# A new hand-written order for a kernel of sliding-window attention and a squared-ReLU feed-forward layer

## The chip, the cores and the metric

The kernel runs on one core of one Trainium2 chip. The metric is the device time of one execution in microseconds (us). Five engines have instruction queues of their own and run them strictly in order: PE (TensorE, matrix products and transposes), DVE (VectorE), ACT (ScalarE), POOL (GpSimd) and SP (SyncE, which only issues transfers here). An instruction that waits for another engine holds up everything behind it on its own engine. Transfers (DMA) are issued by SP, POOL and, once, ACT, and run beside the engines.

## What is computed

Four batches, eight heads, 768 positions, 64 values a head. A query sees the 128 positions up to itself and the first four positions, the sinks. The attention output is laid out as 3072 tokens of 512 values and goes through two products with a squared ReLU between them.

```python
B, H, S, D = q.shape                                   # 4, 8, 768, 64
scores = q @ k.transpose(0, 1, 3, 2) / np.sqrt(D)
pos = np.arange(S)
rel = pos[:, None] - pos[None, :]
keep = (pos[None, :] < 4) | ((rel >= 0) & (rel < 128))
scores = np.where(keep, scores, -1e9)
a = softmax(scores)
x = (a @ v).transpose(0, 2, 1, 3).reshape(B * S, H * D)  # 3072 x 512
h = x @ w_in                                             # 512 x 2048
return np.maximum(h, 0.0) ** 2 @ w_out                   # 2048 x 512
```

Inputs and output are 32-bit floats; the kernel multiplies in bf16.

## The kernel before

**A list of operations and a written order.** The program first builds a list of 946 operations, numbered from 0. An operation is a small function that emits one step: a group of matmuls, one vector or activation instruction, one transfer. It names the engines that may do it, the operations that it follows, and the on-chip rooms that it takes and reads. Nothing of the order is decided by the list. The order is a constant, `ORDER` (line 21), of 946 words, one for each operation. A word is the operation's number, then, where the first engine in the operation's own list is not meant, a letter (`d` DVE, `a` ACT, `g` POOL), then, where an operation may take its PSUM room from either of two pools, `+0` or `+1`. `Plan.run` walks the words from left to right:

```python
o.engine = names[word[-1]] if word[-1] in names else next(iter(o.engines))
for s in o.takes:
    if len(s.pools) > 1:
        s.pool = s.pools[int(chosen.pop(0))]
    s.room = free[s.pool].pop(0)
self.idle = DUMMIES.get(n, 0)
o.run(o.engine)
```

So the order of the words sets two things at once: the order in each engine's queue, and which operation inherits which room, since a room goes to the back of its pool's free list when its last reader has been emitted. Exchanging two neighbouring words of different engines changes no queue. The semaphore waits between engines are derived from the data and from the rooms, so a step that inherits a room waits for the reader that was last in it.

**Rooms.** PSUM has eight banks: the pools `att` and `den` have two rooms of two banks each. SBUF pools: `qr` 5 (loaded q and k), `qs` 6, `expm` 8 (exponentials and other short-lived tiles), `r` 3, `osb` 2 (output), `sg` 4, `u` 2.

**Fillers.** `DUMMIES` (below `ORDER`) gives a few operations extra matmuls on TensorE whose result is not used: 29 in the warm-up at the start (945, line 1363), 8, 10 and 4 ahead of the transposes 58, 63 and 64 (line 185), 3 each ahead of 83, 91 and 97.

**Stages.** The four batches run in a software pipeline: while TensorE works on the layers of batch b, the attention of batch b+1 is interleaved with them.

- *Constants.* DVE fills tiles: 944, 0, 1 (`fill_first`) and 2 (`fill_second`), the last two each three memsets at lines 233 to 235, for the even and the odd batches. POOL builds the identity, triangles and biases (3, 4, 5, line 254) and the head rows (6).
- *Batch 0, loads and head pairs.* q and k of four head pairs come on SP's queue (8 to 15) into `qr`. 7 and 16 to 18 load the sink values; 19, 20, 22, 23, 31 and 32 load v, 21 and 24 to 26 `w_in`, 33 to 36 `w_out`, all on POOL's queue. Each pair's k and q are cast (55, 56 for pair 0; 61, 62; 67, 68; 73, 74), transposed on TensorE (57, 58; 63, 64; 69, 70; 75, 76) and unloaded from PSUM (59, 60; 65, 66; 71, 72; 77, 78; lines 192 on ACT and 194 on DVE).
- *Attention of a token group* (256 positions; three groups per batch). Scores (lines 606 and 613; 83, 84, 91, 92 for group 0, 103, 104, 113, 114 for group 1 of batch 0), exponentials on ACT (line 634), masks on POOL (line 218) or DVE, values (line 682) and a normalisation on DVE (a reciprocal and the product of line 699). The sinks have scores and exponentials of their own (lines 572 and 580; 81, 82 for batch 0, 210, 211 for batch 1, 686, 687 for batch 3) and masked values (79).
- *Turning x.* In batches 0 and 1 TensorE transposes x (99, 101, line 731) and DVE or ACT copies it to `xT` (100, 102). In batches 2 and 3 q and k are loaded by tiles of 128 positions on POOL's queue (line 403; 668 and 669 are the last two q tiles of batch 3) and turned by transfers on SP (line 461; 680 to 683 for the last tiles of batch 3), and x is turned by transfers on SP too (line 713; 486 and 487 for tile group (2,1), 502 and 503 for (2,2), where (2,1) is group 1 of batch 2).
- *Layer 1.* Batch 0: plain products (line 763; 156 is the first), ReLU (line 775 on ACT, 777 on DVE) and square (786). From batch 1 on a block is done with seven products in place of eight: DVE makes sums of `xT` (line 852; 594 to 596 for batch 2), TensorE the products (line 894), DVE subtracts results from a kept copy (line 936; 583 and 585) and adds at the end (line 963; 578), ACT squares.
- *Layer 2.* Two tile groups of batch 0 go by plain products (line 984; 297 and 298 empty group (0,1)); the others by the same seven-product scheme, with sums of the activations on DVE (line 1207; 300 to 303 for group (0,2)) and products on TensorE (line 1233; 304 and 305 for that group). Results are emptied into `osb` and stored by SP. The last group of batch 3 has a form of its own, with three stores (line 1094 and below).

In batch 1 the scores of group 0 are 212 and 219, of group 1 230 and 237; 232, 234, 239 and 241 are masks of group 1, 235 its values. In batch 3, 700, 709 and 716 are values, 701 the normalisation of 700, 727 scores of group 2, 614 the kept copy and 616 a product of a layer-1 block.

## Time and profile before

| | |
|---|---|
| runs of the kernel before | 209.33, 210.71, 211.39 us |
| median of the three | 210.71 us |
| profiled execution, first to last instruction | 208.3 us |
| instructions in it | 5924 |
| bytes moved | 26.10 MB, mean 125 GB/s |
| granted TensorE clock | 1.000 |

The profile is of another execution than the three timed ones. Its page gives busy times per engine, the span in slices, the transfers by queue, the chain of work that ended last, and the costliest groups of instructions by line. A group reads: start time (in a timeline) or busy time, line, engine, operation, the tile that is written and the one that is read with shapes, count, and in brackets the idle time of that engine just before and what ended it. A table of stretches reads: stretch, then length and TensorE's busy time with its count, then weight loads, DVE, ACT and POOL in the same manner, then the granted clock, the mean share of the transfer engines and GB/s.

### The profile page before, as it was taken

The page shows a single profiled execution, that of the slowest core. Times are in us where ns is not written, and L with a number is a line of the kernel's source. Part 1 is how long each engine was busy: PE and PEld are TensorE (multiplying, and loading weights), DVE is VectorE, ACT ScalarE, POOL GpSimd, SP SyncE. Part 2 cuts the span into 40 slices and gives each one's busy share as a digit, 9 for nine tenths or more (in the row PEclk, how much of TensorE's full clock was granted, in tenths as well). Part 3 has the DMA queues.
Part 4 walks back from the last instruction along what each step waited for, and adds up shares of the span by engine and source line. Part 5 has one row for each costly group of instructions (what it writes and reads, how often), then busy time and mean ns, then how long its engine had stood idle before and what let it go on. Part 6 is the DMA issues. An engine that isn't in the chain of part 4 may idle for free.

```text
span 208.3 us, 5924 instructions
## 1 busy us (share of the span) xinstructions
PE 200.5 (96%) x2476; PEld 174.3 (84%) x2476; DVE 173.1 (83%) x318; ACT 135.9 (65%) x189; POOL 96.4 (46%) x138
## 2 busy tenths in 40 slices
PE   7989999999998999999999998999999999999993
PEld 7658997457986889989878987999888999998893
DVE  6759268867599998999999987999989598999933
ACT  2695888433749589999987047988856248693110
POOL 7999274599599976689356209000043000000000
PEclk9999999999999999999999999999999999999999
...
GB/s 190 260 184 207 173 196 215 166 146 142 261 68 148 131 172 137 181 162 121 154 116 220 109 96 134 148 3 0 50 14 145 50 5 113 88 3 0 50 54 201
DMA packets 93994, 26.10 MB, mean 125 GB/s; under 512 B 86800, under 2 KB 91408, under 8 KB 93968
## 3 DMA queue, kind: packets, MB, share of 16 engines
...
q10 hardware_dynamic: 184, 0.14, 0.2%
...
HBM read 27.30 MB, written 6.29 MB: 161 GB/s over the span
## 4 chain that ended last, share of the span: by engine, by line
PE 82%; DVE 5%; DMA 4%; SPq 3%; ACT 2%; issue 2%; DVEq 0%; ACTq 0%
PE py L1233 26%; PE pm L894 23%; PE pm L763 10%; PE py L984 7%; PE po L682 6%; PE ps L613 4%; DMA qr<-in_q_dram 3%; PE pt L507 2%; PE py L1094 2%; SPq L351 2%; DVE t L936 1%; PE px L731 1%; DMA xT<-xn_sb 1%; SPq L461 1%; ACT expm L634 1%
## 5 line engine op out<-in xcount | busy, mean ns | idle before, releaser
L634 ACT ACTIVATE expm<-ps 128x1024 bf16<-128x1024 f32 (+1 forms) x48 | 43.7, 953 | 7.7 <-PE ps L613 7.5
L218 POOL TENSOR_SCALAR_AFFINE_SELECT expm<-expm 128x512 bf16<-128x512 bf16 x34 | 22.7, 705 | 44.2 <-ACT expm L634 40.4
L894 PEld LDWEIGHTS <-w_in_sb 128*128 128x128 bf16 x384 | 32.2, 114 | 2.0 <-issue 1.9
L1233 PEld LDWEIGHTS <-gT_sb 128*128 128x128 bf16 x288 | 27.2, 98 | 4.7 <-issue 1.4
L917 ACT ACTIVATE gT_sb<-r 128x1024 bf16<-128x1024 bf16 x28 | 28.8, 1054 | 2.5 <-DVE r L963 2.3
L894 PE MATMUL pm<-xs,wi 128*128 128x256 bf16 (+1 forms) x288 | 29.2, 246 | 0.1
L192 ACT ACTIVATE osb<-py 128x256 f32<-128x256 f32 (+1 forms) x30 | 11.9, 399 | 25.0 <-PE py L1233 19.8
L936 DVE TENSOR_TENSOR t<-t,pm 128x512 f32<-128x512 f32 x36 | 23.8, 683 | 3.7 <-PE pm L894 2.9
L894 PEld LDWEIGHTS <-wi 128*128 128x128 bf16 x288 | 24.6, 114 | 1.0 <-DVE xs L852 0.4
L1233 PEld LDWEIGHTS <-sg 128*128 128x128 bf16 x216 | 20.3, 98 | 2.7 <-issue 0.5
L963 DVE CUSTOM_DVE_ANT_1 r<-pm,t 128x1024 bf16<-128x1024 f32 x18 | 21.8, 1218 | 0.5 <-PE pm L894 0.5
L763 PE MATMUL pm<-xT,w_in_sb 128*128 128x256 bf16 x192 | 22.0, 273 | 0.0
L763 PEld LDWEIGHTS <-w_in_sb 128*128 128x128 bf16 x192 | 20.6, 114 | 0.3 <-issue 0.2
L894 PE MATMUL pm<-xs,w_in_sb 128*128 128x256 bf16 (+1 forms) x192 | 19.9, 246 | 1.0 <-DVE t L936 1.0
L951 ACT ACTIVATE r<-pm 128x1024 bf16<-128x1024 f32 x16 | 16.3, 1022 | 4.9 <-DVE osb L194 2.3
L1233 PE MATMUL py<-w_out_sb,gT_sb 128*128 128x256 bf16 x144 | 18.7, 273 | 0.6 <-ACT expm L634 0.6
L1233 PE MATMUL py<-wt,sg 128*128 128x256 bf16 x144 | 18.7, 273 | 0.0
L1233 PE MATMUL py<-wt,gT_sb 128*128 128x256 bf16 x144 | 18.5, 273 | 0.0
L682 PEld LDWEIGHTS <-expm 128*128 128x128 bf16 x352 | 16.6, 97 | 1.9 <-issue 0.6
L682 PE MATMUL po<-v,expm 128*128 128x65 bf16 x352 | 17.8, 193 | 0.3 <-ACT expm L634 0.3
L699 DVE TENSOR_TENSOR xn_sb<-po,rc 128x512 bf16<-128x512 f32 (+1 forms) x28 | 17.2, 615 | 1.0
L984 PE MATMUL py<-w_out_sb,gT_sb 128*128 128x512 bf16 x64 | 14.8, 379 | 0.0
(104 smaller groups left out, 376.9 us busy)
## 6 DMA issues: line engine op xcount, KB each, us to landing
...
v<-in_v_dram POOLq DMA_DIRECT2D x24, 128.0 KB, 6.2
qn<-in_k_dram POOLq DMA_DIRECT2D x20, 128.0 KB, 6.1
qn<-in_q_dram POOLq DMA_DIRECT2D x20, 128.0 KB, 6.5
...
```

Of the source, the lines that this page charges most:

```text
L218: nc.gpsimd.affine_select(out=e_tile, in_=e_tile, compare_op=ALU.is_ge, fill=fill, base=i - 1, pattern=[[0, n], [1 if i else -1, 128]], ch ...
L634: nc.scalar.activation(out=x[:, :, o:512], in_=bank_t["s", b, s, m][:, :, o:512], func=AF.Exp, scale=scale)
L682: touch(("po", b, s, m0), e, nc.tensor.matmul(pv[:, i, h2, :], lhsT=lhsT, rhs=rhs, start=(n_ == 0), stop=(n_ == len(mms) - 1)), j)
L699: touch(("po", b, s, m0), e, nc.vector.tensor_tensor(out=xn_sb[:, 2 * s:2 * s + 2, 128 * (m0 + j0):128 * (m0 + j0 + nj)].rearrange("p i (j ...
L763: nc.tensor.matmul(pm[:, i, :], lhsT=w_in_sb[:, fb // 4, kb, fb % 4:512:4], rhs=xT[:, c0 // 256:(c0 + cw) // 256, kb, :], start=(kb == 0), ...
L894: touch(tag, e, nc.tensor.matmul(y[:, bk, i, :], lhsT=weights(name, f0 + i, a), rhs=rhs[:, a, :], start=fresh and i == 0 and a == 0, stop= ...
L917: nc.scalar.activation(out=d, in_=x, func=AF.Square)
L936: touch(tag, e, nc.vector.tensor_tensor(out=T["t"], in0=T["t"], in1=T["y"][:, bk], op=ALU.subtract), bk)
L951: touch(tag, e, nc.scalar.activation(out=r, in_=T["y"], func=AF.Relu), 0, 1)
L963: touch(tag, e, nc.vector._custom_dve(TENSOR_ADD_SAT, out=r.rearrange("p b n c -> p b (n c)"), in0=T["y"].rearrange("p b n c -> p b (n c)" ...
L984: touch((b, u), e, nc.tensor.matmul(pm[:, i, :], lhsT=gT_sb[:, fb, 128 * t:128 * t + 128], rhs=w_out_sb[:, fb, :], start=(fb == 0), stop=( ...
L1233: touch((b, u), e, nc.tensor.matmul(region(name), lhsT=x[:, i, :], rhs=w_[:, i, :], start=first and i == 0, stop=i == HB - 1, skip_group_c ...
```

## The change

Only the constant `ORDER` is replaced by another arrangement of the same 946 words. `DUMMIES`, all functions, tiles and pool sizes stay. In the new order:

- 66 operations go to another engine than before, all of them among DVE, ACT and POOL. Four masks go from DVE to POOL (232, 241, 497, 729) and four from POOL to DVE (265, 474, 499, 724). The casts 56 (DVE) and 74 (ACT) go to POOL; 61, 67, 68 go from DVE to ACT, 73 from ACT to DVE. The rest are unloads, copies, evacuations, ReLUs and squares that go between DVE and ACT, in both directions. DVE has 285 operations where it had 282, ACT 180 where it had 185, POOL 100 where it had 98; PE keeps 321 and SP 60.
- Of the 122 operations that choose a PSUM pool, 23 choose otherwise.
- Words move by a few places nearly everywhere. At the start, `fill_second` (2) moves from the fourth place of DVE's queue to between the normalisation 98 and the copy 102. TensorE transposes k of pair 1 (63) first, then k of pair 0 (57), q of pair 1 (64), q of pair 0 (58), and only then computes the first scores (83); before, it took pair 0, scores 83, then pair 1. On POOL's queue the casts 56 and 74 stand among the first loads.
- The masks 497, 490 and 492 stand ahead of the last q loads of batch 3 (668, 669) on POOL's queue, where the latter stood first;  on SP the turns of x (486, 487, 502, 503) change places with the turns of batch 3 (680 to 683). The subtractions 583 and 585 stand ahead of the sum 594 on DVE, where 594 stood between them.

The diff, cut to the lines at the start and around those places (the whole constant changes):

```diff
 ORDER = """
-944 0 1 2 7 8 9 10 11 12 13 14 15 16 17 18 945+0 3 5 19 20 21 6 79 22 23 24 25 55d 56d 57+0 58 59d 60a 83+0 85 103+1
-105 26 27 28 62d 61d 63+1 64 67d 68d 65a 69+0 70 71d 72d 66a 84+1 73a 74a 75+1 76 78d 91+0 86 77a 93 80 113+1 87+0
-92+1 89 94 95+0 97 115 88 90 96 98 114+1 99+0 101 117 100d 104+0 81+1 102d 107 82 4 29 106g 30 31 32 33 34 35 36 37 38
-39 40 41 42 43 44 45 46 127 47 48 49 50 116d 118d 108d 156+0 109+1 119+1 121 111 162+0 110 120 122 112 123+1 125 124d
...
-474g 669 670 499g 471 522 679 488+0+0 555 554 526 497d 484+1 557 491 489 671 492g 490g
-477+0 500+0 485 478 559 501 561 527+0 528 529d 563 562 493+0 565 558d 494 534 530 535 531d 566+0 567 532 533a 568d 569
-564 570 572 571 536 683 682 677 678 486 502 680 711+0+0 487 503 573 574d 537 538 539d 540 681 541 560 714 712 704+0+0
-580+0 581 576 577 582d 583 594 584 585 575a 705 707 688+0+0 713g 715g 706g 708g 689 691 578 586 587 626+1 627 588a
-628a 612+0 686+0 613 687 630 596 692 690 595 629 631 716+0 717 589a 614a 632 633 579a 634a 635a 615 590 616 597 617
...
+8 0 944 945+0 9 1 55d 5 10 3 11 62d 12 61a 63+0 65 57+0 4 13 7 64 56 59a 14 15 58 19 66 67a 60 20 69+0 73d 21 83+1 68a
+103+1 22 85 71 70 74 23 6 72 24 25 75+0 84+1 77 26 79 76 105 86 91+1 78 93 27 87+0 89 106 92+1 95+1 94 88 90 28 104+0
+97 99+0 80 96 98 2 114+1 101 107 113+1 81+0 29 102 100a 115 117 156+0 30 31 82 109+0 108d 116d 119+1 118d 32 111 110
+121 33 157 34 112 35 122 127 158a 162+1 120 36 163 123+0 125 124a 126 168+0 169 165+0 177+0 164a 37 38 39 166 40 174+1
...
+550 516 521 553 495+0+0 496 551 498 497 527+0 488+0+0 489 483d 491 481d 552d 474d 672 528 555 556 522 673 666 554
+484+0 558 678 561 490 529 685 525 485 562 477+0 492 674 557 564 534 478 563 493+0 530 499d 559 526 667 531d 500+0
+566+0 532 568 501 668 679 494 567 533d 570 486 711+0+0 502 569 535 537 669 571 572 536 573 714 565 538 715 712 503 683
+539 540 574 704+0+0 575 580+0 487 581 576 582d 705 707 682 584 583 585 688+0+0 594 680 577 595 586 689 691 587 626+1
+578 588 627 681 706 713 596 690 628 686+0 670 687 692 612+0 613 630 629 716+0 632 631 717 614 616 708 633 590 579a
...
```

The first removed line of the second part is the end of a longer line of the constant.

More of the change, by code (lines that the diff above doesn't have):

```diff
@@ L21 @@
 ORDER = """
-944 0 1 2 7 8 9 10 11 12 13 14 15 16 17 18 945+0 3 5 19 20 21 6 79 22 23 24 25 55d 56d 57+0 58 59d 60a 83+0 85 103+1
-105 26 27 28 62d 61d 63+1 64 67d 68d 65a 69+0 70 71d 72d 66a 84+1 73a 74a 75+1 76 78d 91+0 86 77a 93 80 113+1 87+0
-92+1 89 94 95+0 97 115 88 90 96 98 114+1 99+0 101 117 100d 104+0 81+1 102d 107 82 4 29 106g 30 31 32 33 34 35 36 37 38
-39 40 41 42 43 44 45 46 127 47 48 49 50 116d 118d 108d 156+0 109+1 119+1 121 111 162+0 110 120 122 112 123+1 125 124d
-126d 157a 163a 158a 164a 168+1 165+0 51 52 53 54 177+0 169a 170d 208g 166a 167a 178d 171+1 179a 172a 128+1 131+0 174+0
@@ L27 @@
-173a 132a 129d 319 323 321 175d 324 176d 322 130a 320 159+1 133a 160a 161a 278+0 279 136+1 144+0 145+0 280 281 148 138
-146 289+1 149d 139d 274 147d 275 282 290 283 291 292 284 276 277 134+1 137+0 135 286a 140 141d 285 287d 293 150+0 151
-294 142+1 196+0 192+1 295 143 193 200+1 198a 202a 195d 197 199d 201 203d 297d 194d 296 298a 152+1 154 204+0 205
-212+0+1 153a 155d 189+0 215 206a 213 190a 214 207d 186+0 216 191d 248+0 187d 249d 251+1 209 253a 188d 252a 180+1 181d
-250d 182d 183+0 326 184a 185d 300 301 230+0+1 233 299 288 219+0+1 231 220 304+0 210+0 306a 211 222 305 237+0+0 240
@@ L32 @@
-232d 325 302 221 303 223 241d 238 239d 311 307 217+1 254+0 224+0 308a 255 309 218 242+0 225 243 452g 422 423 424 425
-426 427 428 429 430 431 432 433 434 234g 235+1 226+0 228 310a 227a 229a 314 236 244+0 246 316a 247a 327 313 245d 329
-256+0+1 257 315 328 332 317 330 347+1 333+1 348 334 259 335a 337 312 336 331 338 349a 263+1+1 266 264 339 351 340 341a
-350 352 435 436 437 258g 438 439 267g 265g 361+0 353 362 354 363d 260g 364 343 365 366 445 440 453 444 441 355a 356a
-342a 448 446 449 442 447 443 451 450 318 344 345 357 375+0 358 376 261+0 359 377a 346a 367 368 379 378 262 380 268+0
@@ L37 @@
-270+0 381 382 360a 369a 271a 269 370d 371 272 273d 372 383a 389 373 463+0+0 385 386 466 464 390 408+0 409 394+1 395
-410a 391 393 387 411 396a 397 412 456+1+0 413 392 414 398 400 415 374d 388a 457 384a 399 504 458 506 465 467 505 508+0
-416a 401 418 419 510a 511 402a 654 655 684g 656 657 658 659 660 661 662 663 664 665 672 459 420 460 685 512a 417a 421a
-403a 404 468+0 509 405 513 454+1 469 406 507 514a 455 515 461+0 472+1+0 407a 517 523 542 462 518 519 521 544 675 673
-470 473 546+0 475 543 548a 479+0+0 516 520d 549 480 482 550a 524 481d 545 476d 525 483d 547 495+1+0 551 553 496 552a
@@ L42 @@
-498 556 674 676 666 667 668 474g 669 670 499g 471 522 679 488+0+0 555 554 526 497d 484+1 557 491 489 671 492g 490g
-477+0 500+0 485 478 559 501 561 527+0 528 529d 563 562 493+0 565 558d 494 534 530 535 531d 566+0 567 532 533a 568d 569
-564 570 572 571 536 683 682 677 678 486 502 680 711+0+0 487 503 573 574d 537 538 539d 540 681 541 560 714 712 704+0+0
-580+0 581 576 577 582d 583 594 584 585 575a 705 707 688+0+0 713g 715g 706g 708g 689 691 578 586 587 626+1 627 588a
-628a 612+0 686+0 613 687 630 596 692 690 595 629 631 716+0 717 589a 614a 632 633 579a 634a 635a 615 590 616 597 617
@@ L47 @@
-693+0 694 591 618 636 619 637 592 598+1 599 620a 600a 638 593a 601 622 640+0 641 602 623 642a 736 643 603 644 604 646
-605 645 709+0 647 624 740+0 639a 621a 606a 648a 742a 649a 607a 608 609 738 737 650 651 743 739 710 610 611d 741
-695+0+0 744a 625a 696 698 652 653d 755 697 699 756 757 745 747 746a 749 748 720+0+0 723 759+0 750 700+0 701 761a 762
-751 721 752a 763a 760 722g 753 724g 727+0+1 774 775 758 728 730 725+0 766 764 778+1 779 765a 729d 767 776 726 777 768
-731g 732+1 733 718 719 702 703 754 734 735 793 794 785 770 769 798+1 812+0 799 813 780a 771a 800a 814a 781 782a 797
@@ L52 @@
-796 786 772 795 815 801 802 816 817 818 803 783 819 784d 787 820a 804 805 789 822 823 829 826 827 828 791 806a 807a
-821a 808 809 788 830+0 831 790a 832a 824 825d 810 858+1 811a 834 872+0 844+1 860a 846a 874a 833 835 836 837 873 845
-859 876 838a 839a 886 887 888 875 877 861 840 841 848 862 864 792 773 842 863 847 889 849 878 879 890+0 865 843a 880a
-850 882 883 851 892a 881a 866d 867d 884 893 894d 868 869 852a 853a 854 855 870 856 895 891 897 896a 885a 900 857d 871d
-905 909+1 899 907 901 924 926 906 898 925 903 911a 912 913a 902a 928+1 904 914 910 929 931+1 915d 908 927 918 920 919
@@ L57 @@
-930a 933a 916 922 921d 934 917 923 932 935 936 939 937 938 943 940 942 941
+8 0 944 945+0 9 1 55d 5 10 3 11 62d 12 61a 63+0 65 57+0 4 13 7 64 56 59a 14 15 58 19 66 67a 60 20 69+0 73d 21 83+1 68a
+103+1 22 85 71 70 74 23 6 72 24 25 75+0 84+1 77 26 79 76 105 86 91+1 78 93 27 87+0 89 106 92+1 95+1 94 88 90 28 104+0
+97 99+0 80 96 98 2 114+1 101 107 113+1 81+0 29 102 100a 115 117 156+0 30 31 82 109+0 108d 116d 119+1 118d 32 111 110
+121 33 157 34 112 35 122 127 158a 162+1 120 36 163 123+0 125 124a 126 168+0 169 165+0 177+0 164a 37 38 39 166 40 174+1
@@ new lines @@
+131+0 41 178 167 159+0 133a 42 43 160 16 128+1 179 175d 132 319 171+1 130 278+0 44 144+0 170 172 129 45 321 136+1
+145+0 46 161a 279 47 148 274 280 146 281 138 289+1 290 48 282 176 134+0 49 139d 147d 322 135 275 137+1 149d 283 173a
+50 140 284 286d 141d 291 276 285 292 324 293 294 51 17 192+1 287 150+0 142+1 194a 193 277 52 195a 295 151 196+0 200+1
+197 199a 143 202a 452 198 296 201 203a 152+1 297d 154 204+0 298d 212+0+1 153a 155 53 215 208 205 189+0 206a 186+0 207
+213 323 248+0 190d 191a 251+1 320 54 187 422 209 180+1 183+0 250 214 252a 216 326 423 253a 184 249 188 181d 182 299
@@ new lines @@
+210+0 185 300 301 211 325 230+1+0 231 219+0+1 304+0 220 302 303 424 233 442 222 288 425 306 305 237+0+0 426 240 328
+427 428 238 221 217+1 307 223 234 218 308 311 224+0 309 429 444 239d 443 310 241 232 254+1 255 242+0 312 225 235+1
+226+0 227a 243 236 228 314 327 229a 244+0 430 431 246 256+0+1 313 432 245 433 446 247a 315 329 333+1 257 317 434 347+1
+435 330 348 259 349d 440 334 316 331 263+1+1 335 336 337 350 351 436 338 266 339 361+0 437 352 264 363d 340 438 341
+353 362 354 355 332 447 365 441 258 356a 342a 364 265d 343 18 344 357 366 358 375+0 345 359 377 376 260 346a 378 267
@@ new lines @@
+367 261+0 379 449 262 380 448 368 268+0 269 270+0 360a 381 369 382 370 450 272 371 372 271a 273 463+0+0 383 385 373
+389 390 451 392 386 464 408+0 387 394+1 409 395 466 410 318 396 439 388a 393 412 391 445 456+1+0 684 411 397 398 413
+414 457 400 374 384a 465 415 654 508+0 655 656 416 657 510 399 504 401 506 402 658 505 467 459 418 419 511 404 468+0
+453 405 659 403a 509 420 469 406 512 458 460 513 660 417a 407 454+0 421a 472+1+0 507 455 473 515 461+0 514 661 546+0
+517 542 462 544 676 677 475 519 662 663 518 548d 479+0+0 543 545 482 470 523 664 520 480 476d 665 549 471 524 547 675
@@ new lines @@
+693+0 615 618 597 694 634 617 591 592 589a 636 598+1 619 637 635a 599 640+0 600 641 620 642 560 638 602 601 709+0 604
+644 639a 603 622 593a 605 623 643 621a 645 606 607a 736 646 624 647 737 648 738 608 609 740+0 741 671 650 651 710 742
+739 743 541 610 625a 649a 695+0+0 744 747 611a 745 652 653 755 759+0 696 757 718 746d 698 756 720+0+0 697 750 699 721
+761d 760 722 700+0 723 749 701 762 748 727+0+0 774 724d 766 702 751 763 764 752 758 703 728 753 765d 768 767 775 730
+754 725+1 778+1 731 770 793 779 776 726 729 769 780 777 771 772 794 732+0 795 781 733 812+0 719 798+1 782d 813 797 814
@@ new lines @@
+734 816 815 796 817 735 783 800d 799 826 784 818 819 802 820 801 788 790 803 822 827 804 823 787 830+0 824 829 785 805
+831 872+0 821a 786 832d 789 806 874d 791 807a 808 825a 809 810 858+1 873 834 833 876 828 773 860 844+1 835 859 862 875
+836 846 861 837 811a 792 877 845 864 878 879 838 839a 847 840 841 863 865 848 886 880 882 866 850 842 849 881a 887 868
+867 890+0 883 843a 851 892 888 884 869 889 893 852 894d 854 870 885a 855 871a 856 891 895 897 853 857 896 900 899 905
+906 907 902d 909+1 901 903 910 924 916 898 911 912 904 913d 925 908 928+0 926 914 929 915d 931+1 917 918 930 932 934
@@ L58 @@
+919 933d 920 927 935 936 939 921 922 937 923 938 940 943 942 941
 """
```

## The prediction

> **What bounds the kernel now.** I read the page first, then the busy time of each engine over stretches cut at TensorE's own gaps, then the timeline of each gap, and for the change I wrote the new order out engine by engine and laid it beside the old one.

> ```profile
> span 208.3 us, 5924 instructions
> PE 200.5 (96%) x2476; PEld 174.3 (84%) x2476; DVE 173.1 (83%) x318; ACT 135.9 (65%) x189; POOL 96.4 (46%) x138
> ```
> ```profile
> 16.59:60.99 44.40, 44.40 (x474) 35.47 (x472) 30.80 (x53) 25.98 (x35) 30.59 (x42) 1.00 1.72 176
> 60.99:65.33 4.34, 3.36 (x43) 2.31 (x44) 4.22 (x7) 4.30 (x7) 4.34 (x6) 1.00 2.20 140
> 65.33:128.26 62.93, 62.78 (x917) 55.78 (x917) 58.41 (x111) 48.84 (x68) 41.06 (x56) 1.00 1.67 142
> 128.26:130.48 2.22, 1.25 (x22) 1.15 (x19) 2.21 (x3) 1.46 (x2) 1.45 (x3) 1.00 0.78 248
> 130.48:203.19 72.71, 72.71 (x838) 67.38 (x837) 64.38 (x111) 44.53 (x63) 4.08 (x6) 1.00 0.16 50
> ```

> In each row of the second fence the first number after the colon is the length, the next TensorE's busy time. TensorE is the bound: between the first layer-1 product (16.59) and the last products it is idle only 0.98 (60.99 to 65.33), 0.15 and 0.97 us (128.26 to 130.48). The new order holds the same matmuls, and after 16.59 nearly the same sequence with neighbours swapped, so it can gain at most these 2.1 us and what the start holds; it can lose in any of some 300 places. DVE is second: 58.41 of 62.93 us busy in the middle.

> **The change part by part.** I sort its parts by stage. The sum is a difference against this execution (208.3 us from first to last instruction); the median of the runs, 210.71, is 2.4 above it, and I add the difference to the median.

> *The start.* Today the scores begin as soon as head pair 0 is there. The new order has TensorE transpose pair 1 first (63), then 57, 64, 58, and only then scores 83; nine casts and unloads swap between DVE and ACT, two casts go to POOL (56, 74), and the second fill (2) moves on DVE from the idle time at the very start to between normalisation 98 and copy 102, on which the first layer-1 product 156 waits.

> ```profile
> 1.27 3.28 PE L1363 MATMUL pw<-tri 128*128 128x128 bf16 x29 [1.27 <-DVE tri L224]
> 2.53 0.61 POOL L254 COPY sg<-sg 128x512 bf16<-128x512 bf16 x1
> 2.71 0.28 DVE L233 MEMSET kblk<- 128x272 uint32 x1
> 3.06 0.49 DVE L234 MEMSET vs<- 128x520 bf16 x1
> 3.68 0.10 DVE L235 MEMSET v<- 128x48 bf16 x1
> 7.02 2.20 DVE L194 CAST qs<-qr 128x512 bf16<-128x512 f32 x4 [1.28 <-DMA qr<-in_q_dram]
> 7.37 1.72 ACT L634 ACTIVATE expm<-ps 128x768 bf16<-128x768 f32 x2 [0.48 <-PE ps L613]
> 7.48 0.73 PE L185 MATMUL pt<-ident 128*128 128x128 bf16 x10
> 9.29 1.29 DVE L194 COPY qkT<-pt 128x512 bf16<-128x512 bf16 x2
> 13.76 3.71 ACT L634 ACTIVATE expm<-ps 128x768 bf16<-128x768 f32 x4
> 15.31 0.42 DVE L699 TENSOR_TENSOR xn_sb<-po,rc 128x256 bf16<-128x256 f32 x1
> 15.68 0.86 DVE L194 COPY xT<-px 128x512 bf16<-128x512 bf16 x2
> 16.16 1.70 POOL L218 TENSOR_SCALAR_AFFINE_SELECT expm<-expm 128x512 bf16<-128x512 bf16 x2
> 16.59 1.91 PE L763 MATMUL pm<-xT,w_in_sb 128*128 128x256 bf16 x16
> 17.37 0.38 ACT L580 ACTIVATE es<-pk 128x256 bf16<-128x256 f32 x1
> ```

> New chain: q of pair 1 lands at 7.02 (DVE waited for it), cast 0.55 (2.20 over 4), four transposes and then 58's eight fillers and four transposes (16 at about 0.056, estimated from 10 in 0.73 less the drain of the last) 0.9 with hand-over, two unloads in a row on DVE 1.3 (9.29 row): 9.8; scores 0.5, less what runs meanwhile: first exponential at about 9.9 against 7.37 now. From there ACT runs five exponentials without the casts, unloads and sink keys that stand between them now, 0.8 to 0.9 each (1.72 for two, 3.71 for four), 4.2 in all: the last ends at 14.1; now it ends one exponential (0.8) after 13.76, at 14.6. Gain about 0.4. Then the fill: 2.71 to 3.78 is 1.07 us, and it stands where DVE now waits only 0.38 (normalisation ends 15.73, second copy starts near 16.11): loss 0.7. Net **+0.3** on 156, bounds -0.7 (q and k land a little earlier, as the first v loads are now queued behind POOL's cast 56) and +1.2. POOL's two casts have no row; a POOL copy of as many elements takes 0.61, a DVE cast 0.55, POOL's mask of the same width 0.85 (1.70 over 2): I take 0.7, near the copy. 74 then has about 0.4 to spare, so 1.2 would cost 0.1.

> Behind 74 on POOL now stand v tile 3, the head rows, w_in 1 to 3, sink values 79, one load and mask 106. That mask moves from 16.16 to about 18.2 and the sink exponential 82 behind two more exponentials and a copy on ACT from 17.37 to about 18.2; first values of the second tile group (109) need both when 156 ends at 18.8. Mask end 18.9 to 19.9: **+0.3**, bounds 0 and 1.0.

> *Into batch 1, and 60.99 to 65.33.*

> ```profile
> 51.28 0.68 DVE L194 COPY osb<-py 128x512 f32<-128x512 f32 x1
> 51.70 0.60 ACT L192 ACTIVATE osb<-py 128x512 f32<-128x512 f32 x1 [0.71 <-PE py L984]
> 59.28 1.23 DVE L777 TENSOR_SCALAR r<-pm 128x1024 bf16<-128x1024 f32 x1
> 61.03 1.02 ACT L775 ACTIVATE r<-pm 128x1024 bf16<-128x1024 f32 x1 [2.63 <-PE pm L763]
> 61.95 2.64 ACT L634 ACTIVATE expm<-ps 128x1024 bf16<-128x1024 f32 x3
> 62.09 0.69 DVE L786 TENSOR_TENSOR gT_sb<-r 128x1024 bf16<-128x1024 bf16 x1
> 63.54 0.69 DVE L1207 TENSOR_TENSOR gT_sb<-gT_sb 128x1024 bf16<-128x1024 bf16 x1
> 64.71 0.43 ACT L580 ACTIVATE es<-pk 128x256 bf16<-128x256 f32 x1
> ```

> Scores 212 take the banks of layer-2 evacuation 298. Today DVE and ACT empty the two halves side by side (51.28, 51.70); in the new order DVE does both, 297 then 298, 0.6 and 0.7, while TensorE has 0.9 of other work left: **+0.3** (0 to 0.6). In the gap at 61 today's path is relu 184 on ACT, one exponential, then product 304 (62.1 + 0.9 = 63.0), and on DVE square and two sums to 64.23, then 305. The new order puts sink exponential 211 (0.43) between relu and exponential, but runs the sink scores in the wait; relu 181 comes behind six other DVE steps instead of three. The DVE chain is unchanged: **+0.2** on 305 (-0.3 to +1.0).

> *The middle.* From the instructions that the row of 65.33 to 128.26 groups (111 on DVE, 917 matmuls) I added up, from 305 on, DVE's work in either order up to the step that each product needs, and TensorE's work up to that product. By the old order the least lead is -0.2 us, by the new one +0.1, and later both keep about 0.7. So the swaps between DVE and ACT cost nothing here; bounds -0.2 and +1.0, as such leads are smaller than one DVE step.

> *128.26 to 130.48.* Sums 594 need xT, turned by DMA, and stand on DVE ahead of subtraction 585 that TensorE awaits.

> ```profile
> 118.21 0.69 DVE L699 TENSOR_TENSOR xn_sb<-po,rc 128x512 bf16<-128x512 f32 x1
> 128.27 0.95 DVE L852 TENSOR_TENSOR xs<-xT 128x512 bf16<-128x512 bf16 x1 [0.64 <-DMA xT<-xn_sb]
> 129.87 0.61 PE L894 MATMUL pm<-xs,w_in_sb 128*128 128x128 bf16 x8 [0.97 <-DVE t L936]
> 131.72 0.40 PE L572 MATMUL pk<-qkT,kblk 128*32 128x512 bf16 x4
> 122.25 2.03 SPq L461 DMA_TRANSPOSE qkT<-qn  x1
> 124.34 2.57 SPq L713 DMA_TRANSPOSE xT<-xn_sb  x2
> ```
> ```profile
> 125.65 2.50 DMA xT<-xn_sb
> ```

> In the new order 585 goes first: **-0.97**. Does another wait follow? The last values of tile group (2,2) come two products (0.87 each) later, so its last normalisation ends near 118.9 + 1.75 + 0.5 + the 0.8 gathered = 122. Then SP issues 502, 503, 683, 487, 682 at 1.25 each (2.57 over 2), where today it is the five turns ahead that delay 503. 487 starts at 125.8 and lands 2.5 later, 128.3; the sums are ready by 129.2, TensorE wants them at 130.31 - 0.97 + 0.8 = 130.1. Fits. 682 lands between 129.5 and 130.4 (issue 1.25 or 2.03); sink scores 686 need it at 131.72 - 0.97 + 0.8 - 0.44 (one product earlier) = 131.1: **+0.2** (0 to 1.0).

> *After 130.*

> Copy 614 (0.60, as the ACT copy of its size at 51.70) reuses the room that values 716 read, and only one product (0.44) is left between 716 and 616, where three were: 0.2. Scores 727 take the bank that normalisation 701 (0.69 at 118.21, an estimated 0.9 with its reciprocal) empties, with one product of 0.87 between, where four lay: 0.25. Together **+0.45** (0.2 to 1.0). The tail keeps its last three products and their chain: 0.

> Sum: 0.3 + 0.3 + 0.3 + 0.2 - 0.97 + 0.2 + 0.45 = +0.8, so 210.71 + 0.8 = 211.5.

> [...] The 29 warm-up matmuls at 1.27 came 0.107 apart (3.28 less a drain), the ten at 7.48 about 0.056 apart. [...] POOL's masks of one size take 1.70 (16.16) and, by two in 2.39 (113.72, quoted below), 1.2; four masks move from DVE to POOL and four back. [...]

> **The rivals.**

> ```profile
> 105.56 0.90 POOL L403 DMA_DIRECT2D qn<-in_q_dram  x1
> 113.72 2.39 POOL L218 TENSOR_SCALAR_AFFINE_SELECT expm<-expm 128x512 bf16<-128x512 bf16 x4
> qn<-in_q_dram POOLq DMA_DIRECT2D x20, 128.0 KB, 6.5
> ```

> 1. *Batch 3's loads come too late* (slower). POOL issues the last q tile of batch 3 (669) at 105.56 now; in the new order it stands behind three masks of tile group (2,2), which end about 116 (113.72 + 2.39), so near 118.3, and lands 6.5 later: 124.8. SP wants to turn it (683) at 124.5, with 487 and 682 queued behind it. From there each microsecond of POOL or DMA delay reaches TensorE after a slack of one. Four late microseconds give +3: 214.5. For: POOL waits in order for ACT's exponentials. Against: the 6.5 is a median over busier stretches (DMA column 1.67 up to 128.26, 0.78 behind it). 0.17.
> 2. *TensorE stays slow in the start*: it idles between the warm-up's end and 6.5, as pair 1 is awaited. If half speed lasts to 10, the 16 transposes and fillers of 64 and 58 cost 0.05 more each and the scores some 0.5: +1.3, 212.8. 0.08.
> 3. *Faster*: the start takes its bound (-0.7 for +0.3, mask free: -1.3), the 0.98 us gap halves, and 682 and the rest fit: about -3.4 on my sum, 208.1. For: all sizes are a few tenths. Against: four terms must agree. 0.12.
> 4. *POOL's masks at 66 to 70*: 241 and 232 move from DVE to POOL behind 234, end at about 70.4 where values 235 want them at 70.5; at 1.7 instead of 1.2 for each of the three: +1.4, 212.9. For: DVE is full here. Against: most masks take 1.2. 0.08.
> 5. *Only the order off TensorE's path differs*: 210.7. 0.05.

> **How the numbers follow.** The forecast, 211.5, has 0.50; its terms' bounds, not all at one end, give 209.8 to 213.2. A change of 1% (2.1 us) is about what a measurement of this kernel can tell from none; that puts the edges at 208.6 and 212.8. Faster: rival 3 and 0.02 of the forecast, 0.14. Slower: rival 1, half of 2 and 4, and 0.13 of the forecast's upper bounds, 0.38. Within: 0.48. The range from 208.8 to 214.8 leaves out most of rival 3 and the far end of rival 1.

> **What would show it.** Right: the first layer-1 product starts at 16.7 to 17.2 with DVE's three memsets just before the second copy; TensorE's gap of 0.97 before the eight matmuls at 129.87 is gone; small idles before 109, 212, 686, 616 and 727. Wrong: a first product before 16.3; xs sums that start after 130; a TensorE gap of more than 1 us anywhere after 66, or DVE idle where TensorE waits for it.

## The result and the profile after

The changed kernel takes 217.21 us (median of four runs, 217.14 to 217.28) against 210.75 before: the ratio is 1.031 with an interval of 1.0253 to 1.0367, so 6.5 us slower. The profiled execution grew by 7.2 us, from 208.3 to 215.5. Most terms of the predicted sum were a few tenths and came out within half a microsecond; the start cost more than forecast, and one place, which the sum put at zero, cost 4.6 us.

First the page of the changed kernel, and its busy times in stretches that begin and end at the same steps as those of before (columns as before: stretch, length, then PE, PEld, DVE, ACT, POOL, then the granted clock).

```profile
span 215.5 us, 5923 instructions
PE 203.3 (94%) x2476; PEld 175.2 (81%) x2476; DVE 176.3 (82%) x321; ACT 135.5 (63%) x184; POOL 95.6 (44%) x140
```
```profile
0.00:18.86 18.86, 14.94 (x176) 10.93 (x177) 11.07 (x31) 10.15 (x15) 14.69 (x31) 0.91 1.20 200
18.86:63.24 44.38, 44.38 (x472) 35.46 (x472) 30.32 (x53) 26.88 (x37) 29.64 (x42) 1.00 1.66 158
63.24:67.52 4.28, 3.25 (x42) 2.26 (x42) 3.75 (x6) 4.24 (x6) 3.12 (x5) 1.00 2.19 140
67.52:79.64 12.12, 9.41 (x139) 7.41 (x138) 10.67 (x17) 4.61 (x9) 12.11 (x16) 0.86 1.59 160
```

The same for before, three of the four rows; the row of 16.59 to 60.99 stands in the prediction:

```profile
0.00:16.59 16.59, 14.28 (x176) 10.73 (x177) 11.10 (x32) 10.82 (x17) 14.87 (x29) 1.00 1.24 211
...
60.99:65.27 4.28, 3.30 (x42) 2.25 (x42) 4.16 (x7) 4.24 (x7) 4.28 (x6) 1.00 2.19 140
65.27:72.81 7.54, 7.54 (x137) 6.65 (x137) 7.40 (x17) 5.00 (x9) 7.49 (x10) 1.00 2.24 138
```

Read in pairs: up to the first layer-1 product 16.59 became 18.86, +2.27. The next 44.4 us are equal to 0.02, and the gap of TensorE behind them is equal, 4.28 and 4.28. The stretch from scores 237 to scores 256 holds the same 14 steps of TensorE in either order; it took 7.54, with TensorE busy all through, and takes 12.12: **+4.58**. What is behind it nets to about +0.4. So 6.9 of the 7.2 us lie in two stretches. In the second the granted clock is 0.86 on average, in the first 0.91, and there are no such values before.

The timeline of the second stretch (start, busy time, line, engine, operation), and below it three windows, show what happens in it:

```profile
69.17 0.90 POOL L402 DMA_DIRECT2D qn<-in_k_dram  x1
...
69.68 3.67 DVE L642 TENSOR_TENSOR expm<-expm,mask 128x768 bf16<-128x768 bf16 x2
...
70.07 2.39 POOL L217 TENSOR_SCALAR_AFFINE_SELECT expm<-expm 128x512 bf16<-128x512 bf16 x4
...
72.94 0.98 PE L681 MATMUL po<-v,expm 128*128 128x65 bf16 x12 [2.60 <-DVE expm L642]
...
73.73 1.90 PE L1232 MATMUL py<-wt,sg 128*128 128x256 bf16 x8
```
```profile
72.94:73.41 0.47, 0.35 (x6) 0.23 (x7) 0.47 (x2) 0.00 (x0) 0.47 (x2) 1.00 1.42 235
73.41:76.83 3.42, 3.42 (x36) 2.42 (x37) 2.49 (x6) 0.73 (x2) 3.42 (x5) 0.50 1.46 98
76.83:79.64 2.81, 2.81 (x61) 2.54 (x58) 2.32 (x6) 1.09 (x2) 2.81 (x4) 1.00 2.01 144
```

Two masks of DVE, 221 and 223, take 3.67 together. Two of the same form earlier in the same run, with no mask of POOL beside them, take 1.02:

```profile
59.46 1.02 DVE L642 TENSOR_TENSOR expm<-expm,mask 128x768 bf16<-128x768 bf16 x2
```

The first of the two, 221, is the long one: 3.20, from 69.68 to 72.89. Beside it POOL runs the four instructions of masks 241 and 232, which the change moved there from DVE, without a gap, at 0.63 to 0.65 each, their quick price. TensorE waits 2.60 for the DVE mask. Then its granted clock is 0.50 for 3.42 us (73.41 to 76.83): the eight matmuls that took 1.04 elsewhere take 1.90.

Rows of TensorE from the start, from where 587 and 612 stand, and from the tail with ACT's row:

```profile
4.65 0.97 PE L184 MATMUL pt<-ident 128*128 128x128 bf16 x10
7.23 0.62 PE L506 MATMUL pt<-ident,qs 128*128 128x128 bf16 x8 [1.60 <-ACT qs L191]
...
9.19 1.06 PE L506 MATMUL pt<-ident,qs 128*128 128x128 bf16 x8
...
12.00 0.62 PE L506 MATMUL pt<-ident,qs 128*128 128x128 bf16 x8
```
```profile
135.25 1.06 PE L893 MATMUL pm<-xs,w_in_sb 128*128 128x128 bf16 x16
...
137.97 0.60 PE L893 MATMUL pm<-xs,wi 128*128 128x256 bf16 x4 [0.46 <-DVE r L962]
```
```profile
206.31 0.38 ACT L191 ACTIVATE osb<-py 128x256 f32<-128x256 f32 x1 [6.80 <-DMA out_dram<-osb]
...
206.75 1.03 PE L1093 MATMUL py<-wt,sg 128*128 128x256 bf16 x8 [0.65 <-ACT osb L191]
```

Eight transposes take 0.62 at 7.23, 1.06 at 9.19 and 0.62 again at 12.00: TensorE was idle from 5.6 to 7.23, while pair 1 was awaited, and ran slow from 8.65 to about 12 (granted clock 0.50 in 10.00 to 12.00). Products 586 and 587 (135.25) follow each other without the old gap of 0.97; 612 (137.97) waits 0.46. In the tail product 932 waits 0.65 for a copy of ACT, and that for a room of the output tile, which a store frees only when it has landed.

### The profile page after: what moved, and what is told of

Same layout as the page of the kernel before. It is cut to its first block, busy times and chain, and to the rows that moved or that the text cites. A ratio compares the mean times of both kernels' runs of the same rounds, so it can differ in the third digit from the quotient of the medians.

```text
span 215.5 us, 5923 instructions
## 1 busy us (share of the span) xinstructions
PE 203.3 (94%) x2476; PEld 175.2 (81%) x2476; DVE 176.3 (82%) x321; ACT 135.5 (63%) x184; POOL 95.6 (44%) x140
## 4 chain that ended last, share of the span: by engine, by line
PE 74%; DVE 12%; DMA 6%; ACT 3%; issue 3%; SPq 1%; ACTq 0%; DVEq 0%
PE py L1232 20%; PE pm L893 20%; PE pm L762 10%; PE po L681 7%; PE py L983 7%; PE ps L612 4%; PE pt L506 3%; DMA qr<-in_q_dram 2%; DMA out_dram<-osb 2%; DVE sg L1206 2%; DVE r L962 2%; DVE expm L642 2%; DVE t L935 2%; DMA xT<-xn_sb 1%; PE px L730 1%
## 5 line engine op out<-in xcount | busy, mean ns | idle before, releaser
L191 ACT ACTIVATE osb<-py 128x256 f32<-128x256 f32 (+1 forms) x26 | 10.1, 393 | 23.8 <-PE py L1232 14.3
L950 ACT ACTIVATE r<-pm 128x1024 bf16<-128x1024 f32 x18 | 18.4, 1022 | 4.9 <-PE pm L893 4.5
L681 PE MATMUL po<-v,expm 128*128 128x65 bf16 x352 | 18.4, 196 | 2.7 <-DVE expm L642 2.6
L893 PE MATMUL pm<-xs,w_in_sb 128*128 128x256 bf16 (+1 forms) x192 | 19.9, 246 | 0.0
L1232 PE MATMUL py<-wt,sg 128*128 128x256 bf16 x144 | 19.5, 281 | 0.0
L698 DVE TENSOR_TENSOR xn_sb<-po,rc 128x512 bf16<-128x512 f32 (+1 forms) x28 | 17.2, 615 | 1.0
L612 PE MATMUL ps<-qkT 64*128 64x128 bf16 (+1 forms) x256 | 14.8, 242 | 0.6 <-ACT es L579 0.6
## 6 DMA issues: line engine op xcount, KB each, us to landing
v<-in_v_dram POOLq DMA_DIRECT2D x24, 128.0 KB, 5.4
qn<-in_k_dram POOLq DMA_DIRECT2D x20, 128.0 KB, 5.8
qn<-in_q_dram POOLq DMA_DIRECT2D x20, 128.0 KB, 5.8
```

What stands on the lines that cost most here:

```text
L612: nc.tensor.matmul(ps[:, h2, o:o + w], lhsT=qkT_sb[r, m, 1, c, :], rhs=qkT_sb[r, m, 0, qb:qb + w // 128, :], start=(i == 0 and not biased) ...
L681: touch(("po", b, s, m0), e, nc.tensor.matmul(pv[:, i, h2, :], lhsT=lhsT, rhs=rhs, start=(n_ == 0), stop=(n_ == len(mms) - 1)), j)
L698: touch(("po", b, s, m0), e, nc.vector.tensor_tensor(out=xn_sb[:, 2 * s:2 * s + 2, 128 * (m0 + j0):128 * (m0 + j0 + nj)].rearrange("p i (j ...
L893: touch(tag, e, nc.tensor.matmul(y[:, bk, i, :], lhsT=weights(name, f0 + i, a), rhs=rhs[:, a, :], start=fresh and i == 0 and a == 0, stop= ...
L950: touch(tag, e, nc.scalar.activation(out=r, in_=T["y"], func=AF.Relu), 0, 1)
L1232: touch((b, u), e, nc.tensor.matmul(region(name), lhsT=x[:, i, :], rhs=w_[:, i, :], start=first and i == 0, stop=i == HB - 1, skip_group_c ...
```

## The experiments

Two theories at the start. **A**: POOL's run of masks holds a DVE instruction beside it, the idle time that follows makes TensorE slow, and the rest of the loss is the start (pair 1 first, fill 2) and 932. **B**: mask 221 is late for a reason of its own, and the moved masks have nothing to do with it. Medians of four runs and ratios to the kernel before on the same chip, with their intervals (ten runs for b_585 and b_start_after). The chips differ: the kernel before ran at 209.92 to 211.04 on them, so a difference of two medians in this table can be off by up to 1 us, and the ratio is the safer number:

| run | edit | median, us | ratio |
|---|---|---|---|
| the change | | 217.21 | 1.031 (1.0253 to 1.0367) |
| a_masks_dve | masks 241, 232 on DVE | 213.61 | 1.0178 (1.0123 to 1.0232) |
| a_load_between | a load between the two masks | 214.94 | 1.0252 (1.0204 to 1.0300) |
| a_429_late | a load from ahead of the masks to behind | 213.92 | 1.0149 (1.0082 to 1.0215) |
| a_221_early | weight sum 328 behind 221, 223 | 214.18 | 1.0193 (1.0160 to 1.0227) |
| a_fill224 | fillers while TensorE waits | 217.60 | 1.0390 (1.0337 to 1.0443) |
| a_fill63 | fillers in the start | 216.68 | 1.0329 (1.0304 to 1.0354) |
| a_fill2_early | fill 2 back | 216.13 | 1.0225 (1.0172 to 1.0277) |
| a_tail | 932 behind 919, 920 | 216.14 | 1.0224 (1.0177 to 1.0271) |
| a_start_before | old start | 216.20 | 1.0290 (1.0249 to 1.0330) |
| a_three | old start, masks on DVE, 932 later | 212.52 | 1.0109 (1.0089 to 1.0129) |
| b_start_after | order before, new start | 211.04 | 1.0051 (1.0020 to 1.0082) |
| b_585 | order before, 585 ahead of 594 | 210.21 | 0.9969 (0.9947 to 0.9992) |
| b_masks_pool | order before, masks 232, 241 on POOL | 225.27 | 1.0666 (1.0616 to 1.0716) |
| b_implant | the same, at another place of POOL's queue | 214.15 | 1.0152 (1.0064 to 1.0240) |

**The two masks back on DVE.**

```diff
-239d 443 310 241 232 254+1
+239d 443 310 241d 232d 254+1
```

> The new order with masks 241 and 232 back on DVE, at the same places of the order. Theory A (the new order loses 4.6 us at 70 us because DVE's mask 221 is held while POOL's four instructions of masks 241 and 232 run, and because TensorE, idle for 2.6 us, then runs at half rate for 3.4 us): mask 221 takes its usual 0.55 us, no half-rate stretch near 73 us; DVE has two more masks of 0.68 to do ahead of values 242 and 235, which may wait 1 to 1.5 us: 213.5 to 215.0. Theory B (mask 221 is held by something else, such as the load that POOL was issuing when it began, or its own input): 221 still takes over 2 us, 217 or more.

213.61, 3.6 below the change by the medians and 2.8 by the ratios. DVE's two masks and the stretch from 237 to 256:

```profile
69.53 1.01 DVE L643 TENSOR_TENSOR expm<-expm,mask 128x768 bf16<-128x768 bf16 x2
```
```profile
67.37:76.66 9.29, 8.57 (x138) 6.67 (x138) 9.12 (x19) 4.54 (x9) 9.29 (x11) 1.00 1.70 157
```

1.01 for two again, no wait of 2.6, the clock at 1.00. Theory B falls as it was put: load 429 is still issued while 221 runs, and alone it holds nothing. The stretch is still 1.75 longer than before (7.54): with the masks on DVE, DVE is busy for 9.12 of 9.29, and the values wait for it. Of that, 0.75 is growth that stayed: POOL's mask 234, which the new order has earlier, now runs beside two sums of DVE, which take 1.00 and 1.11 in place of 0.68 (so they do in the changed kernel).

**A load between the two masks.** Load 430 moves ahead of mask 232 on POOL:

```diff
-310 241 232 254+1 ... 244+0 430 431
+310 241 430 232 254+1 ... 244+0 431
```

> The new order with one load (430) issued by POOL between mask 241 and mask 232. Theory A: DVE's mask 221 gets through when POOL's first mask ends, about 1.2 us earlier, and TensorE's idle time falls from 2.6 to about 1.4 us; 216.0 if the half-rate stretch stays, 214.2 if it goes too. Theory B: mask 221 ends as late as before, 217.2.

The timeline and the stretch:

```profile
69.30 0.90 POOL L403 DMA_DIRECT2D qn<-in_k_dram  x1
...
69.81 3.53 DVE L643 TENSOR_TENSOR expm<-expm,mask 128x768 bf16<-128x768 bf16 x2
...
70.20 1.23 POOL L218 TENSOR_SCALAR_AFFINE_SELECT expm<-expm 128x512 bf16<-128x512 bf16 x2
71.37 0.89 POOL L403 DMA_DIRECT2D qn<-in_q_dram  x1
...
72.11 0.35 PE L682 MATMUL po<-v,expm 128*128 128x65 bf16 x6 [1.63 <-DVE expm L643]
```
```profile
67.64:78.25 10.61, 8.04 (x139) 6.50 (x138) 10.44 (x17) 4.54 (x9) 10.59 (x14) 1.00 2.12 156
```

Mask 221 got through after POOL's first mask, 1.0 us earlier; TensorE waited 1.63 and, behind the second mask, 0.93, and stayed at full clock. 214.94 is between the two values that theory A gave.

**Fillers while TensorE waits.**

```diff
-    945: 29, 58: 8, 63: 10, 64: 4, 83: 3, 91: 3, 97: 3,
+    945: 29, 58: 8, 63: 10, 64: 4, 83: 3, 91: 3, 97: 3, 224: 46,
```

> The new order with 46 filler matmuls ahead of values 224, so that TensorE is busy while it waits for mask 221. Theory A: mask 221 is as late as before, but the matmuls behind 73.4 us no longer take twice as long: 1.9 us less, 215.3. Rival: the slow stretch comes from what delays DVE too (a crowded memory port) and not from TensorE's idle time: it stays, 217.2.

```profile
65.53:76.27 10.74, 10.61 (x184) 9.14 (x184) 10.57 (x17) 4.54 (x9) 10.73 (x14) 1.00 1.53 160
```

The stretch has the 2.7 us of fillers in it and is 1.38 shorter than the changed kernel's 12.12, at a clock of 1.00; DVE's mask takes as long as there. So between these two runs the slow clock goes with TensorE's idle time (2.71 of 12.12 there, 0.13 of 10.74 here), not with what holds DVE. In a_fill63 below, where no slow stretch follows the wait (the clock reads 1.00), the stretch is 10.74 too. But the whole is no faster, 217.60: DVE and POOL met again 2 us behind the stretch, at the sums of `xT` and the next four POOL instructions, and TensorE's waits for DVE behind that (0.94, 0.60 and 0.16) add up to 1.7:

```profile
78.24 2.76 DVE L852 TENSOR_TENSOR xs<-xT 128x512 bf16<-128x512 bf16 x1
78.25 2.46 POOL L218 TENSOR_SCALAR_AFFINE_SELECT expm<-expm 128x512 bf16<-128x512 bf16 x4
```

A sum that takes 0.42 took 2.76. This is another instruction of another form, so the hold does not belong to the mask.

**Fillers in the start.**

```diff
-    945: 29, 58: 8, 63: 10, 64: 4,
+    945: 29, 58: 8, 63: 42, 64: 4,
```

> The new order with 42 instead of 10 filler matmuls ahead of the transposes 63, so that TensorE is busy from the warm-up until q of pair 1 has landed. Theory A (the start loses 2.3 us in all, 1.5 of it because TensorE, idle from 5.4 to 7.2 us, runs at half rate from 8.6 to 12): spacing stays at 0.056 us, the first exponential starts at 10.2 instead of 11.7, the first layer-1 product about 1.5 us earlier: 215.7. Rival (the scores wait for casts and unloads, whatever the rate): first product at most 0.4 us earlier, 216.8 to 217.2.

```profile
4.65 3.52 PE L185 MATMUL pt<-ident 128*128 128x128 bf16 x42
8.01 0.61 PE L507 MATMUL pt<-ident,qs 128*128 128x128 bf16 x8
```

The slow stretch behind 8.65 is gone (the clock reads 1.00 from 5 to 14), as theory A said, and the first layer-1 product came at 18.21 in place of 18.86. The fillers, 42 in 3.52 us (by an estimate from that and the two spacings of the traces, 0.107 each up to 6.7 and 0.056 behind it), ran until 8.0 and so past the time the casts were ready. That is 0.65 earlier, where theory A gave 1.5 and the rival at most 0.4. The result lies between, and how much of the shortfall is the fillers' overrun is not separated. The median is 0.5 lower and the ratio no better (1.0329 against 1.031); what takes the gain back is not shown.

**Fill 2, and product 932.** Two runs, one edit each (a_fill2_early, a_tail):

```diff
-8 0 944 945+0 9 1 55d ... 96 98 2 114+1
+8 0 944 945+0 9 1 2 55d ... 96 98 114+1
```
```diff
-918 930 932 934 919 933d 920 927
+918 930 919 933d 920 932 934 927
```

> The new order with the second fill (2) back behind the first (1) on DVE. Theory A: the copy 102 starts right after normalisation 98, the first layer-1 product 0.6 us earlier (0.56 us of idle time ahead of it goes): 216.6. Rival: the product waits for another input, at most 0.1 earlier: 217.1.

> The new order with the product 932 of the last tile group moved behind the products 919 and 920 of the group before. Theory A: 932 waits 0.65 us because the copy ahead of it, 930, needs an output room that is free only when a store has landed; with two products between, the wait is covered: 0.8 less, 216.4. Rival: 919 or 920 wait in its place, or the store lands later still: 217.2.

216.13 and 216.14, either about what theory A gave, though the intervals of their ratios overlap that of the change; the places themselves show it better. From the end of normalisation 98 to product 156 were 1.46 in the changed kernel (17.40 to 18.86) and 0.95 with the fill moved (15.79 to 16.74): 0.5. In a_tail 932 starts at 207.50 with no wait, behind 919 and 920, which did not wait.

**One part of the change in the order before.** Masks 232 and 241 on POOL (b_masks_pool), and the sums 594 behind 585 (b_585):

```diff
-237+0+0 240 232d 325 302 221 303 223 241d 238 239d
+237+0+0 240 232g 325 302 221 303 223 241g 238 239d
```
```diff
-582d 583 594 584 585 575a
+582d 583 584 585 594 575a
```

> The order before with masks 232 and 241 on POOL instead of DVE. Theory A: a mask of DVE (221 or 223) that runs while POOL's masks run is held for their length, 0.6 to 2.4 us, and TensorE's values 217 or 224 wait for it: 1 to 4 us slower than before; if the two do not meet in time, within 0.5 of before. Theory B (only the new neighbours of mask 221 matter): no DVE mask over 0.7 us, within 0.5 of before.

> The order before with the sums 594 moved behind the subtraction 585 on DVE. By the prediction's term the TensorE gap of 0.97 us at 129.87 goes: 0.97 less than before, 209.8 against 210.75. Rival: the products that need the sums wait instead, within 0.3 of before.

b_masks_pool is 14 us slower, a miss for both theories, and for a reason that neither had: in the old order the third mask of the group, 234, stands on POOL behind thirteen loads, and the two masks, which wait for ACT, hold those loads up. TensorE's row at values 235:

```profile
85.07 0.23 PE L683 MATMUL po<-v,expm 128*128 128x65 bf16 x1 [12.31 <-POOL expm L219]
```

DVE's mask 223 met POOL's mask 241 here (POOL's from 69.01 to 70.77), and was not held to its end:

```profile
69.29 0.98 DVE L644 TENSOR_TENSOR expm<-expm,mask 128x768 bf16<-128x768 bf16 x1
```

It took 0.43 over its price, less than the 0.6 to 2.4 of theory A. The new order puts 234, 241 and 232 among the loads; the old one could not take them. b_585 is faster than both kernels, by 0.3% of the kernel before (0.1 to 0.5% by the interval), where the term gave 0.5%; TensorE goes from product 586 to 587 at once:

```profile
129.76 1.08 PE L895 MATMUL pm<-xs,w_in_sb 128*128 128x128 bf16 x16
```

**The start alone, both ways; and all three undone.** a_start_before takes the words up to 156 from the old order, b_start_after the other way about; a_three adds the edits of a_masks_dve and a_tail to a_start_before.

```diff
-8 0 944 945+0 9 1 55d 5 10 3 11 62d 12 61a 63+0 65 57+0
...
-97+0 99+0 80 96 98 2 114+1 101 107 113+1 81+0 29 102 100a 115 117 156+0
+944 0 1 2 7 8 9 10 11 12 13 14 15 16 17 18 945+0 3 5 19 20 21 6 79 22 23 24 25 55d 56d 57+0 58 59d 60a 83+0
...
+39 40 41 42 43 44 45 46 127 47 48 49 50 116d 118d 108d 156+0
```

> The new order with the start of the order before: all words up to and with the first layer-1 product 156 as they stood before, the rest as in the new order. Theory A (the start costs 2.3 us of the 6.5, independent of what follows): first product at 16.6 to 17.5, mask 221 still held near 3.2 us, 214.9. Rival (what the start loses is made up by a later wait in any case): 216.5 or more.

> The order before with the start of the new one, all words up to and with 156. Theory A: the first layer-1 product 2.3 us later than before (18.9 in place of 16.6, less where pair 1 lands early), 211.0 + 2.3 = 213.3 at most, 211.5 at least. Rival: the later stages have slack that takes it up, 211.

> The new order with the start of the order before, masks 241 and 232 on DVE, and product 932 behind 919 and 920. Theory A (these three places hold all that the new order loses): 217.2 - 2.3 - 3.6 - 0.7 = 210.6, equal to the order before within 0.5. Rival (other losses of the new order were hidden behind these): 212 or more.

The start is worth less than the two first profiles say: 1.0 us in one direction (a miss; 0.4 by the ratios) and 0.9 in the other, where 2.3 was expected at most and 0.5 at least. It varies from run to run. In the six profiled runs with the old start the first layer-1 product is at 16.59, 16.91, 16.97, 17.17, 17.47 and 18.05; in the eight with the new one, untouched, at 16.87, 17.90, 17.99, 18.23, 18.71, 18.83, 18.86 and 18.99. The means are 17.2 and 18.3, so +1.1, and the two profiles compared above stand near opposite ends. The four latest of the eight (18.71 to 18.99) have a mean of 18.85, the other four (16.87 to 18.23) one of 17.75: 1.7 and 0.6 later than the old start. Among the four latest are the changed kernel and a_masks_dve (18.71), and in both TensorE's transposes start about 0.107 apart for a time, eight in 1.06 from 9.19 and from 9.36; how much of the 1.1 between the two halves is this slow stretch is not shown. a_three comes to 1.1% above before, not to zero: the rival's value (212 or more), not theory A's 210.6. The stretch from 237 to 256 is as in a_masks_dve:

```profile
66.04:75.33 9.29, 8.57 (x137) 6.67 (x137) 9.12 (x19) 4.54 (x9) 9.29 (x11) 1.00 1.76 163
```

1.75 of the 2.3 that remain are there: the new order's sequence on DVE in this stretch, with the hold taken out and the 0.75 beside mask 234 left in.

**Which DVE instruction is held.** Weight sum 328 behind masks 221 and 223:

```diff
-305 237+0+0 426 240 328 427 428 238 221 217+1 307 223 234 218
+305 237+0+0 426 240 427 428 238 221 217+1 307 223 328 234 218
```

> The new order with the weight sum 328 moved from ahead of masks 221 and 223 to behind them on DVE, so that 328 meets POOL's masks 241 and 232. Theory A (POOL's run of masks holds whichever DVE instruction meets it): 221 and 223 take 0.5 to 1.0 each, 328 takes 2.5 to 3.3 in place of 0.69, TensorE no longer waits at values 224 but at 242 for mask 239, which stands behind 328: 216.5 to 217.2. Rival (it is the form of mask 221, with its mask read again for each head, that is held): 328 takes 0.7 to 1.2, 213.5 to 214.5.

```profile
67.78 1.89 DVE L643 TENSOR_TENSOR expm<-expm,mask 128x768 bf16<-128x768 bf16 x2
69.58 1.11 DVE L818 TENSOR_TENSOR w_in_sb<-w_in_sb 128x1024 bf16<-128x1024 bf16 x1
```

Nothing was held for long: masks and sum took 0.43 more each, about two thirds of one POOL instruction. 214.18, and the stretch 9.14. These are the rival's figures (328 at 0.7 to 1.2, 213.5 to 214.5), but not by its reason: the masks have the form that it names and were not held either, and in a_fill224 a sum of another form was. So it is not any DVE instruction beside POOL's masks that is held to their end.

That left the question of what ahead of mask 221 matters. In the changed kernel it begins while POOL issues load 429, right ahead of the four instructions. Two runs were made for it: 429 behind the masks on POOL, nothing else moved (a_429_late); and the same neighbourhood put into the old order, with masks 232 and 241 between loads 431 and 432 (b_implant).

```diff
-309 429 444 239d 443 310 241 232 254+1
+309 444 239d 443 310 241 232 429 254+1
```
```diff
-240 232d 325 302 221 303 223 241d 238 239d ... 243 452g 422 ... 431 432 433
+240 325 302 221 303 223 452g 422 ... 431 232g 241g 432 238 239d ... 243 433
```

> The new order with the load 429 moved on POOL's queue from ahead of masks 241 and 232 to behind them; the same instructions, none on another engine. Theory C (mask 221 is held for four POOL instructions because it begins while POOL issues a load right ahead of them; a DVE instruction that begins while a mask runs gets in at the next break): 221 begins while mask 234 or 241 runs and takes at most 1.1 us, TensorE does not wait 2.6 us at 224, 213.5 to 215.0. Theory A (any run of POOL masks holds mask 221 to its end): 221 takes 2 us or more, 216.5 or more.

> The order before with masks 232 and 241 on POOL, between the loads 431 and 432, with no load of the queue moved behind mask 234 that did not stand there. By the trace of before, mask 223 would begin on DVE some 0.15 us before the load 431 is issued and the four POOL instructions follow. Theory C: 223 takes 2.4 to 3.0 us in place of 0.55, values 224 and 242 wait for it and for mask 239 behind it, 211.5 to 213.0 against 210.4. Rival (the hold belongs to the new order's neighbours): 223 takes 0.5 to 1.0, and DVE has two masks less to do: 209.5 to 210.5.

```profile
66.28 5.42 POOL L218 TENSOR_SCALAR_AFFINE_SELECT expm<-expm 128x512 bf16<-128x512 bf16 x6 [1.16 <-issue]
```
```profile
68.73 1.89 DVE L643 TENSOR_TENSOR expm<-expm,mask 128x768 bf16<-128x768 bf16 x2
```
```profile
66.56:75.71 9.15, 8.04 (x138) 6.50 (x138) 8.98 (x17) 4.54 (x9) 9.10 (x11) 1.00 1.25 139
```

a_429_late takes 213.92, as the expectation gave (its theory C is that the load issue right ahead of the masks decides): one load issue moved by two words on POOL gives back 3.3 us. The edit also lets POOL's masks begin earlier against DVE, so it does not separate the load from the moment. Six POOL instructions in a row now take 5.42, 0.9 each in place of 0.65, and DVE's two masks take 0.43 more each (1.89 together in place of 1.02): both sides are longer, and neither is held to the other's end. b_implant is a miss, in its time and for theory C. The masks came 0.15 us behind the start of mask 223, which then ran in its usual 0.55, while POOL's four took 3.11 in place of 2.39. It is slower than before for another reason, seen in b_masks_pool too: mask 234 ends up behind, and values 235 wait for it.

```profile
73.92 0.20 PE L683 MATMUL po<-v,expm 128*128 128x65 bf16 x1 [2.24 <-POOL expm L219]
```
```profile
66.19:78.35 12.16, 9.54 (x138) 8.06 (x138) 7.03 (x16) 5.05 (x9) 10.78 (x14) 0.86 1.75 131
```

Here too the clock falls to 0.86 on average after the wait.

## Why the prediction was wrong, step by step

The forecast was +0.8 and the range ended at 214.8; measured is +6.5.

**The step that failed** is "the middle": "So the swaps between DVE and ACT cost nothing here; bounds -0.2 and +1.0". It added up DVE's work at the durations of the old trace and found that DVE kept its lead. The durations did not hold. The old trace had a sign of it: the sum at 128.27 in the prediction took 0.95 beside POOL's masks, where sums of its size take 0.42 elsewhere, and 0.95 was used as its price. The change moved masks 241 and 232 beside DVE's mask 221, whose price went from 0.55 to 3.20. Of the 4.58 us of this stretch the runs separate three parts: 1.6 is the new sequence with POOL's and DVE's instructions each some tenths longer beside the other (9.15 in a_429_late against 7.54; five steps of DVE take 0.2 to 0.4 more each there, 1.8 together, and what the sequence would cost without them is not shown), 1.6 the hold (10.74 in a_fill224, where TensorE is kept busy, against 9.15), and 1.4 the slow clock (12.12 against 10.74). The first part alone is already beyond the term's upper bound. One of the prediction's own signs of being wrong, "a TensorE gap of more than 1 us anywhere after 66", is there: 2.60.

**Rival 4 had the place and the wrong victim.** It put the danger at masks 241 and 232 at 66 to 70 and priced POOL's masks at 1.7 in place of 1.2. POOL's ran at 0.65 an instruction, 1.2 a mask, their cheap price, while DVE's mask 221 took 3.20. The rival priced the meeting on POOL's side only. In the traces of the kernel before and of the changed kernel, the DVE instructions that grow by 0.2 us or more beside POOL's masks (by 0.20 to 0.54, and mask 221 by 2.66) all have two SBUF operands, and those that read one from PSUM (the normalisations of 128x512 at 0.69, the subtractions of line 935 at 0.67 to 0.69) keep their length. Which of the two goes first, and for how long, is not shown: mask 221 began 0.39 ahead of POOL's first instruction and ended behind its fourth.

**The start** was +0.3 with bounds -0.7 and +1.2. In the two profiles it is +2.27; over the profiled runs it is +1.1, and by the ratio of b_start_after 0.4 to 1.7, about the upper bound of the term. Its parts: the fill was put at 0.7 and costs 0.5 to 0.6; the slow clock of rival 2, put at +1.3 with a chance of 0.08, did occur, from 8.65 to 12 here, and a_masks_dve has transposes as far apart (about 0.107), but what it costs alone is not shown; the step of the scores, which was to begin at 9.8, began at 10.04, but the first exponential started at 11.68 where 9.9 was forecast, and the last of the five exponentials ended at 16.31 where 14.1 was forecast.

**The other terms.** TensorE's gap of 0.97 ahead of 587 is gone, as forecast. The wait at 61 is equal, where +0.2 was given. The waits at 109, 212, 616 and 727, worth 0.3, 0.3 and 0.45, did not come at all, so 1.05 of the forecast slowdown was not there; at 686 there was none, but 612 right behind it waits 0.46 for the final sum 578, a wait that no term named. Batch 3's loads (rival 1) were in time.

**The tail** was put at 0: "keeps its last three products and their chain". The three products are the same, but 932 lost the three products (920, 919, 916) that stood directly ahead of it and covered the landing of the store: 0.65, and 1.13 in the profile of a_start_before.
